# Attention over 16 blocks on one core: four engines' programs as loops with register addresses, and the second half of each V block loaded one block later

## The chip, the cores and the metric

The kernel runs on one core of a Trainium2 chip. Five engines work side by side, each with its own program, and wait for each other only by semaphores: TensorE (PE in the profile) multiplies, VectorE (DVE) transposes, reduces and takes reciprocals, ScalarE (ACT) computes activations (exponentials and scaled copies), GpSimd (POOL) clears a buffer, SyncE (SP) issues transfers. PEld is TensorE's loading of weights. Sixteen DMA engines move data between HBM and the on-chip memory (SBUF); TensorE writes to PSUM, whose banks hold 512 float32 for each of 128 partitions.

The metric is the time of one execution in microseconds, as the device measures it. A profiled execution also has a span, from its first instruction to its last.

## The reference

```python
B, H, Sq, Skv, Dh = 8, 16, 16, 2048, 256
def reference(q, k, v):                    # bfloat16; q: (8,16,16,256), k and v: (8,16,2048,256)
    scale = q.shape[-1] ** -0.5
    scores = jnp.einsum('bhqd,bhkd->bhqk', q, k) * scale
    attn = _softmax(scores, axis=-1)
    return jnp.einsum('bhqk,bhkd->bhqd', attn, v)
```

There are 128 heads. Each has 16 queries and its own 2048 keys and values of 256 numbers, so K and V are 134 MB each, and every byte of them is used by 16 queries only. Q and the output are 1 MiB each.

## The kernel before, in words

**Tiling.** Eight heads make a block g, 0 to 15; their 8 x 16 queries are the 128 rows of the block's scores. Four heads make a unit: block g has units e = 0 and 1. A unit of K or V is 8192 rows of 256 numbers, 64 rows in a line for each of 128 partitions, so its load, K(g,e) or V(g,e), is 4 MiB in 128 runs of 32 KiB (`load`, L97). The tensor SL has four slots of that size, called KA, KB, VA, VB. K(0,0) and K(0,1) are put into VA and VB, all other K into KA and KB; V goes into VA and VB, but for block 15, whose V goes into KA and KB, in two pieces and in eight.

**The steps for one block**, with the names that are used below:
- T(g,e): VectorE transposes unit e of K in place, seen as float32 pairs, in blocks of 32 x 32 (L154, four instructions; two of them are a half unit).
- QK(g,e): TensorE multiplies the unit by the scaled queries, 32 products of 128 x 512 in two groups of 16, one for each half of the unit (`qk`, L234 with a load of weights and L235 without). Both units add into the same four banks, S_ps. The weights QW hold the queries of a unit's four heads at those heads' rows and zeros elsewhere; ScalarE writes them (L174, four copies for each block).
- Maximum (VectorE, L156), exponentials with their sums (ScalarE, L206, two halves), transposes of P (VectorE, L162, two halves), sum and reciprocal (VectorE, L164 and L166).
- Copies: ScalarE places the transposed P of one head after the other into PTz, a buffer of zeros (L219, eight copies, four for each unit).
- PV(g,e): TensorE multiplies 64 columns of PTz by the unit of V, 64 products of 128 x 256 (`pv`, L251), into a bank O_ps for each unit.
- Evacuation: ScalarE scales the result by the reciprocal (L180, 64 rows for each unit), and its queue stores 64 KiB (L184).

**Order.** All programs are written out by hand. VectorE runs, for each block, T(g,0), T(g,1), maximum, transposes of P, sum and reciprocal. TensorE runs QK of block 0 and then a loop over g = 1 to 15: QK(g,0), QK(g,1), PV(g-1,0), PV(g-1,1); PV of block 15 follows. ScalarE runs, for block g, the weights of g+1, the exponentials, the evacuations and the store of g-1, and the eight copies of g. Only TensorE's program has a loop; the others are straight code for 16 blocks.

**The queue of loads.** One queue, SyncE's, issues Q, K(0,0), K(0,1), and then for g = 1 to 15: K(g,0), K(g,1), V(g-1,0), V(g-1,1). Each load waits for its slot: K(g,e) until QK(g-1,e) is done (`c_qk`), V(g,e) until PV(g-1,e) is done (`c_pv`); a load that waits holds up all behind it. Since K(0) lies in VA and VB, K(1) can be issued at once, and V(0,e) waits for QK(0,e).

Of the kernel before, what the change touches and what calls it, by code (L numbers as in the profile page):

```python
# [4 lines left out]
ACTF = mybir.ActivationFunctionType  # L5
ALU = mybir.AluOpType
AX = mybir.AxisListType
PE = mybir.EngineType.PE
BF16 = mybir.dt.bfloat16
# [3 lines left out]
KA, KB, VA, VB = 0, 1, 2, 3  # L13


def bass_standalone__softmax_full_bidir__sampling_kernel(
# [17 lines left out]
    qh = q.rearrange("b h s d -> (b h) (s d)")  # L34
    oh = out.rearrange("b h s d -> (b h s) d")

    with ExitStack() as es:
# [5 lines left out]
        PTc = ec(nc.sbuf_tensor("PTc", [128, T, 32], BF16))  # L43
        PTz = ec(nc.sbuf_tensor("PTz", [128, 2, T, 128], BF16))
        O_fin = ec(nc.sbuf_tensor("O_fin", [128, 2, D], BF16))
        negm = ec(nc.sbuf_tensor("negm", [128, G], F32))
        lsum = ec(nc.sbuf_tensor("lsum", [128, G, 2], F32))
        ltot = ec(nc.sbuf_tensor("ltot", [128, G], F32))
        rinv = ec(nc.sbuf_tensor("rinv", [128, G], F32))

        S_ps = ec(nc.psum_tensor("S_ps", [128, 4, 512], F32))
        O_ps = ec(nc.psum_tensor("O_ps", [128, 4, 512], F32))
# [4 lines left out]
        s_q = sem("s_q")  # L57
        s_k = [sem("s_ka"), sem("s_kb")]
        s_k0 = [sem("s_k0a"), sem("s_k0b")]
        s_v = [sem("s_va"), sem("s_vb")]  # L60
        s_st = [sem("s_st%d" % i) for i in range(2)]
# [4 lines left out]
        c_kt = [[sem("c_kt%d%d" % (e, h)) for h in range(2)] for e in range(2)]  # L66
        c_qk = [sem("c_qka"), sem("c_qkb")]
# [5 lines left out]
        c_pv = [sem("c_pv0"), sem("c_pv1")]  # L73
        c_pl = sem("c_pl")
# [4 lines left out]
        def ap_of(t_ap, offset, dims):  # L79
            return bass.AP(tensor=t_ap.tensor, offset=offset, ap=[list(t_ap.ap[0])] + [list(d) for d in dims])  # L80


        TAIL = [(0, 19), (19, 14), (33, 10), (43, 7), (50, 5), (55, 4), (59, 3), (62, 2)]
        TAIL_A = [(0, 37), (37, 27)]
        s_tail = [sem("s_t%d" % i) for i in range(len(TAIL))]
        s_vl = [sem("s_vl%d" % i) for i in range(len(TAIL_A))]
        s_vc = sem("s_vc")
        s_kl = sem("s_kl")

        def obank(g, e):  # L90
            return e + (2 if g == last else 0)

        def kslot(g, e):
            return (VA, VB)[e] if g == 0 else (KA, KB)[e]
# [3 lines left out]

        def on_sync(eng):
            eng.dma_start(QT[:], qh).then_inc(s_q, 16)  # L100
            for e in range(2):
                load(eng, ku, 0, e, kslot(0, e), 0, T, s_k0[e])
            for g in range(1, G):
                for e in range(2):
                    if g >= 2:
                        eng.wait_ge(c_qk[e], g)
                    if (g, e) != (last, 1):
                        load(eng, ku, g, e, kslot(g, e), 0, T, s_k[e])
                    else:
                        load(eng, ku, g, e, kslot(g, e), 0, 32, s_k[e])  # L110
                        load(eng, ku, g, e, kslot(g, e), 32, 32, s_kl)
                w = g - 1
                for e in range(2):
                    if w:
                        eng.wait_ge(c_pv[e], w)
                    else:
                        eng.wait_ge(c_qk[e], 1)
                    if (w, e) != (last - 1, 1):
                        load(eng, vu, w, e, (VA, VB)[e], 0, T, s_v[e])
                        if e:  # L120
                            eng.sem_inc(s_vc, 16)
                    else:
                        load(eng, vu, w, e, VB, 0, 32, s_v[e])
                        load(eng, vu, w, e, VB, 32, 32, s_vc)

            eng.wait_ge(c_qk[0], G)
            for (a, n), s in zip(TAIL_A, s_vl):
                load(eng, vu, last, 0, KA, a, n, s)
            eng.wait_ge(c_qk[1], G)
            for (a, n), s in zip(TAIL, s_tail):  # L130
                load(eng, vu, last, 1, KB, a, n, s)
            eng.wait_ge(c_ev, 2 * last + 2)
            eng.dma_start(oh[128 * last:128 * last + 128, :], O_fin[:, last % 2, :]).then_inc(s_fin, 16)
            eng.wait_ge(s_fin, 16)

        def on_gpsimd(eng):
            eng.memset(PTz[:].rearrange("p a t c -> p (a t c)").bitcast(F32), 0.0).then_inc(c_pool, 1)  # L137

        def on_vector(eng):
# [4 lines left out]
            for g in range(G):  # L144
                for e in range(2):
                    for c in range(4):
                        if g == 0 and c == 0:
                            eng.wait_ge(s_k0[e], 16)
                        elif c == 0:
                            eng.wait_ge(s_k[e], 16 * g)  # L150
                        elif (g, e, c) == (last, 1, 2):
                            eng.wait_ge(s_kl, 16)
                        x = SLf[:, kslot(g, e), 16 * c:16 * c + 16, :].rearrange("p t i -> p (t i)")
                        eng.transpose(x, x).then_inc(c_kt[e][c // 2], 1)  # L154
                eng.wait_ge(c_qk[1], g + 1)
                eng.tensor_reduce(out=negm[:, g:g + 1], in_=S_ps[:].rearrange("p c n -> p (c n)"),  # L156
                                  axis=AX.X, op=ALU.max, negate=True).then_inc(c_mx, 1)
                for h in range(2):
                    eng.wait_ge(c_ex[h], g + 1)
                    if g and h == 0:  # L160
                        eng.wait_ge(c_cp, 8 * g)
                    eng.transpose(PTc[:, 32 * h:32 * h + 32, :].rearrange("p t x -> p (t x)"),  # L162
                                  P_sb[:, 1024 * h:1024 * h + 1024]).then_inc(c_pt, 1)
                eng.tensor_reduce(out=ltot[:, g:g + 1], in_=lsum[:, g, :], axis=AX.X, op=ALU.add).then_inc(c_ri, 1)  # L164
                eng.wait_ge(c_ri, 2 * g + 1)
                eng.reciprocal(rinv[:, g:g + 1], ltot[:, g:g + 1]).then_inc(c_ri, 1)  # L166

        def on_scalar(eng):
            def qwb(g):
                Q, r = g // 4, g % 4  # L170
                for a in range(4):
                    dv = QW[32 * a:32 * a + 32, 0, 16 * a, :]
                    sv = QT[32 * Q:32 * Q + 32, :]
                    eng.activation(ap_of(dv, dv.offset, [[1024 + 512, 2], [2, 64], [1, 2]]),  # L174
                                   ap_of(sv, sv.offset + 2 * (8 * r + a), [[8, 2], [64, 64], [1, 2]]),
                                   ACTF.Copy, scale=scale).then_inc(c_qw, 1)

            def evac(g, e):
                rows = slice(64 * e, 64 * e + 64)
# [6 lines left out]
            def finish(g):  # L186
                eng.wait_ge(c_ri, 2 * g + 2)
                if g >= 2:
                    eng.wait_ge(s_st[g % 2], 16 * (g // 2))
# [128 lines left out]
```

## Time and profile before

| | us |
|---|---|
| median of 3 runs | 635.95 (635.76 to 636.34) |
| profiled execution | 636.1 |
| its span | 634.8 |
| PE busy | 488.3 (77%) |
| VectorE busy | 365.2 (58%) |
| ScalarE busy | 214.8 (34%) |
| DMA | 270.64 MB, 426 GB/s over the span |

In a row of the timeline stand start and length in us, engine, line, operation, what it writes and reads, the number of instructions put together, and in square brackets how long the engine was idle before and what ended that. A row of windows has the stretch, its length, the busy time of PE, PEld, DVE, ACT and POOL with the number of instructions, TensorE's granted clock, the mean busy share of the 16 DMA engines, and GB/s. A row of the issues of DMA ends with the KB of one transfer and the us from its issue to its landing. In a row of queues stand packets, MB and share of time. SPq is SyncE's queue of transfers.

### The profile page before, as it was taken

The page shows a single profiled execution, that of the slowest core. Times are in us where ns is not written, and L with a number is a line of the kernel's source. Part 1 is how long each engine was busy: PE and PEld are TensorE (multiplying, and loading weights), DVE is VectorE, ACT ScalarE, POOL GpSimd, SP SyncE. Part 2 cuts the span into 40 slices and gives each one's busy share as a digit, 9 for nine tenths or more (in the row PEclk, how much of TensorE's full clock was granted, in tenths as well). Part 3 has the DMA queues.
Part 4 walks back from the last instruction along what each step waited for, and adds up shares of the span by engine and source line. Part 5 has one row for each costly group of instructions (what it writes and reads, how often), then busy time and mean ns, then how long its engine had stood idle before and what let it go on. Part 6 is the DMA issues. An engine that isn't in the chain of part 4 may idle for free.

```text
span 634.8 us, 6396 instructions
## 1 busy us (share of the span) xinstructions
PE 488.3 (77%) x3072; PEld 274.9 (43%) x2560; DVE 365.2 (58%) x210; ACT 214.8 (34%) x289; POOL 7.1 (1%) x5
## 2 busy tenths in 40 slices
PE   0738989595896958869597795967959689595998
PEld 0202828154271532716336262452724527144287
DVE  2968583763738546294562945739366393663830
ACT  1042252525035250342513325142252322524170
POOL 4000000000000000000000000000000000000000
PEclk9978999798997989969799797998979989798899
DMA  8999999999999999999999999999999999999997
GB/s 376 436 441 432 428 432 432 430 430 431 432 429 434 429 432 433 429 434 429 433 430 429 432 429 433 430 430 433 434 429 436 433 433 432 432 432 425 430 425 285
DMA packets 13113, 270.64 MB, mean 426 GB/s; under 512 B 1456, under 2 KB 3760, under 8 KB 4400
## 3 DMA queue, kind: packets, MB, share of 16 engines
q1 hardware_dynamic: 10944, 269.55, 98.8%
q10 hardware_dynamic: 2160, 0.98, 0.5%
q8 instruction: 3, 0.05, 0.0%
q14 instruction: 6, 0.05, 0.0%
HBM read 269.48 MB, written 1.05 MB: 426 GB/s over the span
## 4 chain that ended last, share of the span: by engine, by line
DMA 58%; PE 23%; DVE 16%; ACT 2%; issue 0%; SPq 0%
DMA SL<-in_k_dram 58%; DVE SL L154 15%; PE S_ps L234 11%; PE S_ps L235 10%; PE O_ps L251 2%; ACT PTz L219 1%; DVE PTc L162 1%; DVE negm L156 1%; ACT P_sb L206 0%; ACT O_fin L180 0%; SPq L97 0%; SPq L100 0%; DVE rinv L166 0%; DVE ltot L164 0%
## 5 line engine op out<-in xcount | busy, mean ns | idle before, releaser
L154 DVE STREAM_TRANSPOSE SL<-SL 128x2048 f32<-128x2048 f32 x128 | 284.2, 2279 | 157.9 <-DMA SL<-in_k_dram 157.9
L234 PE MATMUL S_ps<-SL,QW 128*128 128x512 bf16 x512 | 214.0, 418 | 143.5 <-DVE SL L154 143.3
L251 PE MATMUL O_ps<-SL,PTz 128*128 128x256 bf16 x2048 | 226.3, 273 | 0.9 <-ACT PTz L219 0.7
L234 PEld LDWEIGHTS S_ps<-SL,QW 128*128 128x128 bf16 x512 | 75.1, 147 | 326.6 <-issue 171.7
L251 PEld LDWEIGHTS O_ps<-SL,PTz 128*128 128x128 bf16 x2048 | 199.8, 98 | 30.9 <-issue 4.5
L235 PE MATMUL S_ps<-SL,QW 128*128 128x512 bf16 x512 | 212.5, 415 | 0.0
L219 ACT ACTIVATE PTz<-PTc 32x1024 bf16<-32x1024 bf16 x128 | 134.9, 1054 | 11.3 <-ACT O_fin L180 5.9
L174 ACT ACTIVATE QW<-QT 32x256 bf16<-32x256 bf16 x64 | 26.8, 419 | 243.3 <-PE S_ps L235 236.2
L156 DVE TENSOR_REDUCE negm<-S_ps 128x1 f32<-128x2048 f32 x16 | 36.7, 2292 | 61.4 <-PE S_ps L235 61.4
L180 ACT ACTIVATE O_fin<-O_ps,rinv 64x256 bf16<-64x256 f32 x32 | 15.0, 468 | 137.6 <-PE O_ps L251 137.5
L162 DVE STREAM_TRANSPOSE PTc<-P_sb 128x1024 bf16<-128x1024 bf16 x32 | 37.9, 1224 | 20.3 <-ACT P_sb L206 20.3
L206 ACT ACTIVATE P_sb<-S_ps,negm 128x1024 bf16<-128x1024 f32 x32 | 35.3, 1109 | 25.5 <-DVE negm L156 25.5
L137 POOL MEMSET PTz<- 128x8192 f32 x1 | 6.9, 6924 | 0.3 <-POOLq L303 0.3
L206 ACT ACTIVATION_READ_ACCUMULATOR P_sb<-S_ps,negm 128x1 f32 x32 | 6.3, 196 | 0.0
L143 DVE STREAM_TRANSPOSE QT<-QT 128x2048 f32<-128x2048 f32 x1 | 2.3, 2312 | 3.7 <-DMA QT<-in_q_dram 3.7
L166 DVE RECIPROCAL rinv<-ltot 128x1 f32<-128x1 f32 x16 | 2.6, 164 | 0.5
L164 DVE TENSOR_REDUCE ltot<-lsum 128x1 f32<-128x2 f32 x16 | 1.8, 112 | 0.0
L174 ACT ACT_TABLE_LOAD x1 | 1.3, 1283 | 0.7 <-PEq L303 0.7
L140 DVE MEMSET QW<- 128x1024 f32 x1 | 0.9, 912 | 1.0 <-PEq L303 1.0
L303 POOL MEMSET const-bfloat16-1.0<- 128x1 bf16 x1 | 0.1, 101 | 0.0
L303 POOL MEMSET const-uint8-127<- 128x1 uint8 x1 | 0.1, 101 | 0.0
L303 POOL MEMSET const-float32-0.0<- 128x1 f32 x1 | 0.1, 98 | 0.2 <-issue 0.2
(1 smaller groups left out, 0.1 us busy)
## 6 DMA issues: line engine op xcount, KB each, us to landing
SL<-in_k_dram SPq DMA_DIRECT2D x31, 4096.0 KB, 25.8
SL<-in_v_dram SPq DMA_DIRECT2D x29, 4096.0 KB, 29.1
SL<-in_k_dram SPq DMA_DIRECT2D x2, 2048.0 KB, 23.7
SL<-in_v_dram SPq DMA_DIRECT2D x2, 2048.0 KB, 29.2
SL<-in_v_dram SPq DMA_DIRECT2D x1, 2368.0 KB, 21.6
SL<-in_v_dram SPq DMA_DIRECT2D x1, 1728.0 KB, 25.4
SL<-in_v_dram SPq DMA_DIRECT2D x1, 1216.0 KB, 20.7
QT<-in_q_dram SPq DMA_DIRECT2D x1, 1024.0 KB, 4.9
```

What stands on the lines that cost most here:

```text
L137: eng.memset(PTz[:].rearrange("p a t c -> p (a t c)").bitcast(F32), 0.0).then_inc(c_pool, 1)
L154: eng.transpose(x, x).then_inc(c_kt[e][c // 2], 1)
L156: eng.tensor_reduce(out=negm[:, g:g + 1], in_=S_ps[:].rearrange("p c n -> p (c n)"), axis=AX.X, op=ALU.max, negate=True).then_inc(c_mx, 1)
L162: eng.transpose(PTc[:, 32 * h:32 * h + 32, :].rearrange("p t x -> p (t x)"), P_sb[:, 1024 * h:1024 * h + 1024]).then_inc(c_pt, 1)
L166: eng.reciprocal(rinv[:, g:g + 1], ltot[:, g:g + 1]).then_inc(c_ri, 1)
L174: eng.activation(ap_of(dv, dv.offset, [[1024 + 512, 2], [2, 64], [1, 2]]), ap_of(sv, sv.offset + 2 * (8 * r + a), [[8, 2], [64, 64], [1, 2]]),
L180: eng.activation(O_fin[rows, g % 2, :], O_ps[rows, obank(g, e), 0:D], ACTF.Copy, scale=rinv[rows, g:g + 1]).then_inc(c_ev, 1)
L206: eng.activation(P_sb[:, 1024 * h:1024 * h + 1024], S_ps[:, 2 * h:2 * h + 2, :].rearrange("p c n -> p (c n)"), ACTF.Exp, bias=negm[:, g:g ...
L219: eng.activation(PTz[32 * a:32 * a + 32, z, :, 64 * e + 16 * a:64 * e + 16 * a + 16], sv[:, :, 16 * (a % 2):16 * (a % 2) + 16], ACTF.Copy) ...
L234: return eng.matmul(dst, w, x, start=start, stop=stop)
L235: return eng.add_instruction(mybir.InstMatmult(name=nc.get_next_instruction_name(), engine=PE, start_tensor_calc=start, stop_tensor_calc=stop,
L251: ins = eng.matmul(O_ps[:, bank, 0:D], PTz[:, z, t, :], SL[:, slot, t, :], start=(t == 0), stop=(t == T - 1))
```

## The change

- SyncE, ScalarE and VectorE get loops over the blocks (`nc.Fori`), with addresses and the values of waits computed in registers, and branches (`If_ne`, `If_lt`) for what the first or last block does otherwise. GpSimd gets increments that raise some semaphores at the start, so that one formula serves all blocks. TensorE keeps one loop for all of its work after QK of block 0, now with PV inside for every block; QK of block 0 is two nested loops with 8 products in a round, after four products that clear S_ps with the zeroed PTz as both operands. QK(0,0) and QK(0,1) each wait for the whole of T.
- T takes two instructions for a unit instead of four.
- Q is loaded with other rows on the partitions: partition 32a + u holds head 4u + a, so that ScalarE can address a block's queries with one register. The source's dimensions are 4 x 32 x 4096 instead of 128 x 4096.
- V's second unit goes one block later: the queue's order is K(j,0), K(j,1), V(j-2,1), V(j-1,0), and TensorE's is QK(r,0), QK(r,1), PV(r-2,1), PV(r-1,0). For j = 2 there is no V(0,1) to issue (it was issued before), so that K(2,0), K(2,1), V(1,0) and K(3,0) follow each other.
- Both units of PV now add into one bank, and one evacuation of 128 rows follows PV(g,1). PV(g+1,0) waits for it. ScalarE's order is: weights of the next block, exponentials of g, evacuation of g-2, copies of unit 1 of g-1, store of g-2, copies of unit 0 of g. VectorE's transposes of P of block g wait for the copies of unit 1 of g-1, since PTc is one buffer. VectorE's order in a round is: maximum, transposes of P, sum and reciprocal of g, then T of g+1.
- V(14,1), V(15,0) and V(15,1) are loaded in 3, 2 and 8 pieces, all into VA and VB; each piece waits until PV has passed its columns, counted in steps of 16 columns. Results stay in O_fin for all blocks.

```diff
-KA, KB, VA, VB = 0, 1, 2, 3
+VA, VB, KA, KB = 0, 1, 2, 3
+C = 16
...
-    qh = q.rearrange("b h s d -> (b h) (s d)")
+    qh = q.rearrange("b h s d -> (b h) (s d)").rearrange("(u a) n -> a u n", a=4)
...
+        PIECES = {(last - 1, 1): [(0, 16), (16, 14), (30, 34)], (last, 0): [(0, 37), (37, 27)],
+                  (last, 1): [(0, 16), (16, 14), (30, 11), (41, 8), (49, 6), (55, 4), (59, 3), (62, 2)]}
...
+        def k_and_v(eng, j, es):
+            for e in range(2):
+                eng.wait_ge(c_qk, 8 * j + 4 * e - 4)
+                load(eng, ku, j, e, KA + e, 0, T, s_k[e])
+            for e in es:
+                w = j - 1 - e
+                eng.wait_ge(c_pv, 8 * w + 4 * e + 4)
+                load(eng, vu, w, e, VA + e, 0, T, s_v[e])
...
         def on_sync(eng):
             eng.dma_start(QT[:], qh).then_inc(s_q, 16)
...
+            for j in range(2, 3):
+                k_and_v(eng, j, (0,))
+            with nc.Fori(3, last, engines=[SP]) as j:
+                k_and_v(eng, j, (1, 0))
...
         def on_vector(eng):
...
+            for e in range(2):
+                eng.wait_ge(s_k0[e], 16)
+                for h in range(2):
+                    kt(e, h, VA + e)
+            with nc.Fori(0, G, engines=[DVE]) as g:
+                eng.wait_ge(c_qk, 8 * g + 8)
...
                 for h in range(2):
                     eng.wait_ge(c_ex[h], g + 1)
-                    if g and h == 0:
-                        eng.wait_ge(c_cp, 8 * g)
+                    if h == 0:
+
+                        eng.wait_ge(c_cp, 8 * g + 9)
...
+                with eng.If_lt(gg, last):
+                    for e in range(2):
+                        for h in range(2):
+                            if h == 0:
+                                eng.wait_ge(s_k[e], 16 * g + 16)
+                            elif e:
+                                eng.wait_ge(s_kl, 16 * ((g + 2) >> 4) + 1)
+                            kt(e, h, KA + e)
...
         def on_scalar(eng):
...
+            with nc.Fori(0, G, engines=[ACT]) as g:
+                eng.wait_ge(c_qk, 8 * g + 8)
+                qwb((g + 1) & 15)
                 eng.wait_ge(c_mx, g + 1)
...
+                with eng.If_ne(g2, 0):
+                    evac(n)
+                with eng.If_ne(gg, 0):
+                    eng.wait_ge(c_pv, 8 * g)
+                    copies(1)
+                with eng.If_ne(g2, 0):
+                    store(n, (g + 14) & 15)
                 eng.wait_ge(c_pt, 2 * g + 2)
+                eng.wait_ge(c_pv, 8 * g + 4)
+                copies(0)
...
         def on_tensor(eng):
...
+            with nc.Fori(0, 2, engines=[PE]) as e:
+                with nc.Fori(0, 4, engines=[PE]) as b:
+                    eng.wait_ge(c_kt, 2 * e + 2)
+                    for par in range(2):
+                        for c in range(4):
+                            ins = mm(S_ps[:, c, :], QW[:, e, :, 2 * b + par], SLk[:, VA + e, c, b, par, :, :],
+                                     False, False, c == 0, False)
+                    ins.then_inc(c_qk, 1)
...
+            with nc.Fori(1, G + 2, engines=[PE]) as r:
+                rr = eng.to_reg(r)
+                with eng.If_lt(rr, G):
+                    for e in range(2):
+                        for h in range(2):
+                            eng.wait_ge(c_kt, 4 * r + 2 * e + h + 1)
+                            if e + h == 0:
+                                eng.wait_ge(c_ex[1], rr)
+                            ins = qk(e, (2 * h, 2 * h + 1), KA + e)
+                        ins.then_inc(c_qk, 4)
+                with eng.If_ne(rr, 1):
...
+                    eng.wait_ge(c_cp, 8 * r + 1)
+                    eng.wait_ge(s_v[1], 16 * (r - 1))
+                    pv(1, lambda t: lim2 if t in dict(PIECES[(last - 1, 1)]) else lim1)
+                with eng.If_lt(rr, G + 1):
+                    lim = eng.to_reg((r & 16) + 1)
+                    eng.wait_ge(c_ev, rr)
+                    eng.wait_ge(c_cp, 8 * r + 5)
+                    eng.wait_ge(s_v[0], 16 * r)
+                    pv(0, lambda t: lim)
```

258 lines of the change are left out of this document (98 added, 160 removed).

## The prediction

> K(g,e), V(g,e), T, QK, PV, "copies" and "evacuation" are the loads and steps named in the section on the kernel before.
>
> **What bounds the kernel now.** I read the page first, then long and short windows, the queue's waits, one block's timeline, the start and the end.
>
> ```profile
> span 634.8 us, 6396 instructions
> ...
> PE 488.3 (77%) x3072; PEld 274.9 (43%) x2560; DVE 365.2 (58%) x210; ACT 214.8 (34%) x289; POOL 7.1 (1%) x5
> ...
> q1 hardware_dynamic: 10944, 269.55, 98.8%
> ...
> q8 instruction: 3, 0.05, 0.0%
> ...
> DMA 58%; PE 23%; DVE 16%; ACT 2%; issue 0%; SPq 0%
> ```
>
> The queue that brings K and V (q1) is busy 98.8% of the span, and no engine is over 77%. In the chain of waits (last line) most of the time is one transfer after another.
>
> ```profile
> 100.00:600.00 500.00, 392.35 (x2456) 219.74 (x2046) 291.90 (x168) 171.54 (x230) 0.00 (x0) 0.90 1.00 431
> 631.00:631.50 0.50, 0.50 (x7) 0.45 (x5) 0.00 (x0) 0.00 (x0) 0.00 (x0) 1.00 0.08 29
> ```
>
> Through the middle 500 us all 16 DMA engines are busy (share 1.00, the column before the last) at 431 GB/s, 27 for each. So a 4 MiB load takes 4.194 MB / 431 GB/s = 9.73 us and a block (four loads, 38.9, and its store) 39.0. The second row says that by 631.5 the stream has nearly run out.
>
> ```profile
> SPq L97 <- PE S_ps L235: 392.1, 32, 25.8
> SPq L97 <- PE O_ps L251: 185.9, 28, 7.0
> ```
>
> The issuing queue waits long (total, times, longest), but that costs nothing while loads issued earlier still move. The time is therefore: first byte, stream, any time in which all four slots are taken and nothing moves, and what follows the last byte.
>
> ```profile
> 346.37 8.61 ACT L219 ACTIVATE PTz<-PTc 32x1024 bf16<-32x1024 bf16 x8 [0.41 <-ACT O_fin L180]
> 347.91 8.89 DVE L154 STREAM_TRANSPOSE SL<-SL 128x2048 f32<-128x2048 f32 x4 [10.23 <-DMA SL<-in_k_dram]
> ...
> 362.54 8.31 SPq L97 DMA_DIRECT2D SL<-in_k_dram  x2
> ...
> 370.32 14.13 PE L251 MATMUL O_ps<-SL,PTz 128*128 128x256 bf16 x128
> ...
> 370.52 2.29 DVE L156 TENSOR_REDUCE negm<-S_ps 128x1 f32<-128x2048 f32 x1 [3.84 <-PE S_ps L235]
> ...
> 374.08 2.37 DVE L162 STREAM_TRANSPOSE PTc<-P_sb 128x1024 bf16<-128x1024 bf16 x2 [1.27 <-ACT P_sb L206]
> ...
> 376.53 0.16 DVE L166 RECIPROCAL rinv<-ltot 128x1 f32<-128x1 f32 x1
> ...
> 377.59 0.47 ACT L180 ACTIVATE O_fin<-O_ps,rinv 64x256 bf16<-64x256 f32 x1 [2.44 <-PE O_ps L251]
> ```
>
> One block (start and length in us). T takes 8.89 for a unit; VectorE is idle 10.23 before it, because K arrives late, not the engine. From the end of QK (370.52) to the evacuation (377.59) are 7.07, the 64 products of a unit's PV.
>
> **The change part by part.**
>
> *Q's load.* Its source was 128 rows in one dimension and becomes 4 x 32 rows, with the 4 outermost. In the kernel before q1 carries 76 transfers (74 loads, Q, the last store) of 128 rows each: 76 x (128 + 16) = 10944, the count above. So each is one packet for a row and one closing packet for each of 16 engines: rows are dealt out along the outermost dimension. No row shows an outermost 4. One end of its price is nothing:
>
> ```profile
> QT<-in_q_dram SPq DMA_DIRECT2D x1, 1024.0 KB, 4.9
> ...
> 0.00:1.70 1.70, 0.00 (x0) 0.00 (x0) 0.68 (x1) 0.96 (x1) 1.17 (x5) 1.00 0.00 0
> 1.70:2.50 0.80, 0.00 (x0) 0.00 (x0) 0.23 (x1) 0.32 (x1) 0.80 (x1) 1.00 0.71 143
> ...
> 0.74 0.38 SPq L100 DMA_DIRECT2D QT<-in_q_dram  x1
> ```
>
> The other end is 4 engines: 1.049 MB at 4 x 27 GB/s = 9.7 us where 16 take 2.4, so +7.3 for all that is queued behind it on those four. I take 7.3, since 4 entries can't be dealt to 16 engines in the way that the count shows. A load has landed when its slowest engine has, so K(0,0) comes 7.3 later. (The issue at 0.74 and the empty first window give about 1.0 us from issue to first byte.) [...]
>
> *First products.* QK(0,0) began after half of its unit; now it waits for the whole unit, in two nested loops of 8 products a round.
>
> ```profile
> 15.34 8.89 DVE L154 STREAM_TRANSPOSE SL<-SL 128x2048 f32<-128x2048 f32 x4 [7.39 <-DMA SL<-in_k_dram]
> ...
> 19.99 0.62 PE L234 MATMUL S_ps<-SL,QW 128*128 128x512 bf16 x1 [19.99 <-DVE SL L154]
> 20.41 0.63 PE L235 MATMUL S_ps<-SL,QW 128*128 128x512 bf16 x1
> ...
> 25.05 8.89 DVE L154 STREAM_TRANSPOSE SL<-SL 128x2048 f32<-128x2048 f32 x4 [0.82 <-DMA SL<-in_k_dram]
> ...
> 37.78 2.29 DVE L156 TENSOR_REDUCE negm<-S_ps 128x1 f32<-128x2048 f32 x1 [3.84 <-PE S_ps L235]
> ...
> 42.21 0.20 ACT L206 ACTIVATION_READ_ACCUMULATOR P_sb<-S_ps,negm 128x1 f32 x1
> ...
> 43.87 17.64 DVE L154 STREAM_TRANSPOSE SL<-SL 128x2048 f32<-128x2048 f32 x8
> ```
>
> Before: T(0,0) from 15.34, first product 19.99, T(0,1) to 33.94, QK(0,1) done 37.78, that is 3.84 later.
>
> ```profile
> 74.79 8.90 DVE SL L154 x4
> 83.69 0.05 issue
> ...
> 84.18 0.22 PE S_ps L235
> ...
> 87.51 26.38 DMA SL<-in_k_dram
> ```
>
> [...] Now T(0,0) runs 22.6 to 31.5, and QK(0,0) takes 9 x 0.42 + 23 x 0.22 = 8.8, to 40.3, or 40.7 with 0.1 for each of four loop ends. T(0,1) runs 32.35 to 41.25; QK(0,1) takes the 3.84 of a half, 16 x 0.22 for the other and 0.4 for loop ends: done at 49.0. Loop ends aren't in the trace: nothing to 0.38 each (the queue's issue at 0.74 is the nearest instruction without data), which gives 48.6 to 50.8. The four products that clear the scores and GpSimd's increments come before K(0,0) and are hidden by it.
>
> *V's second unit one block later.* After V(0,1) the queue has K(2,0), K(2,1), V(1,0) and then K(3,0): three loads instead of four ahead of K(3,0), since V(1,1) waits for PV(0,1), now behind QK(2,1). And the copies of unit 1 move from the end of their block to behind the next block's exponentials, ahead of its transposes of P, which T waits for on VectorE. From QK(0,1) done: T(1,0) 43.87 - 37.78 = 6.1, and 0.2 for a branch; T of both units 17.64; half of QK 3.84: QK(1,1) at +27.8. Maximum and exponentials 42.41 - 37.78 = 4.6; branches 0.2; four copies 4.3 (half of 8.61); transposes of P 2.4; sums and a branch 0.5: T(2,0) at +39.8 = 88.8. QK(2,0) ends 12.7 (74.79 to 87.51) to 14.6 (347.91 to 362.54) after T begins; with the middle, 13.7, at 102.5. There K(3,0) is issued; first byte 103.5.
>
> ```profile
> 72.32 0.33 SPq L97 DMA_DIRECT2D SL<-in_v_dram  x1
> ...
> SL<-in_v_dram SPq DMA_DIRECT2D x1, 4096.0 KB, 22.1
> ```
>
> The ninth load, V(1,0), landed at 72.32 + 22.1 = 94.4; with Q's delay at 101.7. Its last byte moves 0.9 sooner (K(0,0): 15.34 less 1.7, less 5.24 MB at 431 GB/s, less 0.5 for the weak second window). From 100.8 all four slots are full, with K(2,0), K(2,1), V(1,0) and V(0,1), and the stream stands still: 2.7 us. The bounds 48.6 with 12.7 and 50.8 with 14.6 give 1.3 and 5.4. Everything later shifts by 7.3 + 2.7 = 10.0, on all engines: the twelve that Q didn't delay only stand longer.
>
> *Later blocks.* T(3,0) comes at +76.6 = 125.6, QK(3,0) ends at 139.3, K(4,0)'s first byte is at 140.3; the stream has work until 103.5 + 38.9 = 142.4. Room 2.1, so no second stall. The loop of dependences is now T 17.64, half of QK 3.84, PV 7.07, evacuation 0.47, branches 0.3, copies 4.3, transposes of P 2.4, sums and branch 0.5: 36.5 us. Against 39.0 it gains 2.5 a block on K(3,0)'s lead (landed 114.1, used 125.6) and waits for data from about block 8. Some 15 register instructions and branches lie on it; they may cost 2.5 / 15 = 0.17 us each beyond my 0.05 (the "issue" piece at 83.69) before they bind. Looping on ScalarE, VectorE and the queue costs nothing while this room lasts, and its whole length in each of 12 blocks without it (rival D). Waits added beside this path: PV(g-1,0) waits for the evacuation of block g-2 (one bank now), so PE is done at 370.5 + 7.07 + 0.65 + 7.07 = 385.3, and next has a half unit of K at 386.9 + 4.4 (the next block begins 39.0 after 347.91): hidden by 6. Behind PV(g-1,0) ScalarE's copies of unit 0 end at 389.6, its next work is at 409.5. One evacuation of 128 rows for two of 64 saves 0.47 where ScalarE was idle: nothing.
>
> *The end.*
>
> ```profile
> 582.41 17.66 DVE L154 STREAM_TRANSPOSE SL<-SL 128x2048 f32<-128x2048 f32 x8 [10.26 <-DMA SL<-in_k_dram]
> ...
> 618.53 14.15 PE L251 MATMUL O_ps<-SL,PTz 128*128 128x256 bf16 x128 [0.69 <-ACT PTz L219]
> ...
> 632.71 0.47 ACT L180 ACTIVATE O_fin<-O_ps,rinv 64x256 bf16<-64x256 f32 x1 [6.44 <-PE O_ps L251]
> ```
>
> Before: 128 products from 618.53 to 632.68, behind the stream's end; 2.1 us of evacuation and store follow, to 634.8. Now K(15) is a load earlier and the products wait for their piece of V: last byte 631.4, landed 0.4 later (an estimate, half of the 0.9, for a small piece), last products 0.4, then 2.1: 634.3, so -0.5. PE's own chain, with T(15,0) at 582.41 - 9.73 and 17.8 for both units: 590.5 + 3.84 + 5 x 7.07 + 0.65 for each of two evacuations = 631.0, hidden by the data, barely; uncovered, the -0.5 shrinks to 0.
>
> *Sum.* 634.8 + 7.3 + 2.7 - 0.5 = 644.3 of span. The profiled execution took 636.1, 1.3 outside its span: 645.6. The median of the runs, 635.95, is 0.15 lower, which I leave out.
>
> **The rivals.**
>
> B: Q still runs on 16 engines. Only the stall and the end remain: 636.1 + 2.7 - 0.5 = 638.3. For it: the 4.9 us. Against it: the 4 in front.
>
> C, not slower: the stream never stands still. It decides at K(3,0)'s issue: before 92.5 without Q's delay, so QK(0,1) done by 92.5 - 53.5 = 39.0, 1.2 after the old 37.78. Starting QK(0,0) at half a unit would nearly do it; waiting for whole units can't by the rows above, and Q at 16 engines is needed too. 636.1 - 0.5 = 635.6; it is faster by more than a measurement can tell only if the uneven last microsecond of the stream goes as well, somewhat under half of its chance.
>
> D: the loops' own instructions bind every block. At 0.3 us for each of 15 the loop of dependences is 36.0 + 4.5 = 40.5; from 125.6 twelve of them end at 612, where K(15,0) landed at 582.7: +29, so 675. For it: only PE had a loop before. Against it: PE's loop goes round 15 times here, and its instruction queue (q8) moved 3 packets in all. [...]
>
> **How the numbers follow.** A, the forecast, 0.74; B 0.11; C 0.07; D 0.08. A's own range: Q 7.3 +- 0.6, stall 1.3 to 5.4, end -0.5 to 0, so 643.6 to 649.4. The range takes in B, and a weak D above: 637.5 to 651; C and most of D are left out. 0.2% is 1.3 us, about what a measurement of this kernel can tell from no change. Faster 0.03 and same 0.04 are C; slower 0.93 is the rest.
>
> **What would show it.** Q landing near 13 instead of 5.6, and 77 x 144 - 12 = 11076 packets on q1 (one load is cut into one piece more; Q has 12 closing packets fewer). T(0,0) at 22.6; QK(0,1) done at 49; a hole of about 3 us in DMA between 100 and 105, and none later; VectorE waiting some 2 us for K in the late blocks; the end 2.9 us after the last piece. The prediction is wrong if Q lands before 6 (B), if there is no hole (C), or if VectorE never waits for K in late blocks (D).

## The result and the profile after

| | before | after |
|---|---|---|
| median of 6 runs each | 636.06 us (635.76 to 636.34) | 663.76 us (663.06 to 664.64) |
| ratio after / before | | 1.0436, 95% interval 1.0423 to 1.0449 |
| profiled execution, its span | 636.1, 634.8 | 664.4, 662.9 |

The change makes the kernel 27.7 us slower; 9.7 were forecast. The page of the kernel after, engines, queues and the chain of waits:

```profile
span 662.9 us, 7353 instructions
...
PE 497.0 (75%) x3076; PEld 271.6 (41%) x2545; DVE 361.0 (54%) x146; ACT 209.1 (32%) x277; POOL 7.1 (1%) x5
...
q1 hardware_dynamic: 11076, 269.55, 97.0%
...
q8 instruction: 1, 0.02, 0.0%
...
DMA 42%; PE 33%; DVE 18%; issue 4%; ACT 3%; ACTq 1%; SPq 0%; DVEq 0%
```

PE is busy 9 us longer than before, the other engines no longer, the same bytes move, and q1 has the 11076 packets that were forecast, so Q does run on four engines. The start is another matter. VectorE's timeline of the kernel after:

```profile
30.40 2.31 DVE L145 STREAM_TRANSPOSE QT<-QT 128x2048 f32<-128x2048 f32 x1 [28.46 <-DMA QT<-in_q_dram]
39.85 8.77 DVE L149 STREAM_TRANSPOSE SL<-SL 128x4096 f32<-128x4096 f32 x2 [7.15 <-DMA SL<-in_k_dram]
...
66.29 2.29 DVE L157 TENSOR_REDUCE negm<-S_ps 128x1 f32<-128x2048 f32 x1 [7.96 <-PE S_ps L244]
```

Q lands at 30.4 (forecast: near 13) and T(0,0) starts at 39.85, 24.5 us later than the 15.34 of before. The windows of the first 30 us say what happens meanwhile, first of the kernel after, then of the kernel before (the last two numbers are the DMA engines' busy share and GB/s):

```profile
2.00:5.00 3.00, 0.00 (x0) 0.00 (x0) 0.00 (x0) 0.02 (x1) 3.00 (x1) 1.00 0.91 183
5.00:10.00 5.00, 0.00 (x0) 0.00 (x0) 0.00 (x0) 0.00 (x0) 3.60 (x1) 1.00 1.02 210
10.00:15.00 5.00, 0.00 (x0) 0.00 (x0) 0.00 (x0) 0.00 (x0) 0.00 (x0) 1.00 1.11 193
15.00:20.00 5.00, 0.00 (x0) 0.00 (x0) 0.00 (x0) 0.00 (x0) 0.00 (x0) 1.00 1.12 177
20.00:25.00 5.00, 0.00 (x0) 0.00 (x0) 0.00 (x0) 0.00 (x0) 0.00 (x0) 1.00 0.87 136
25.00:30.00 5.00, 0.00 (x0) 0.00 (x0) 0.00 (x0) 0.00 (x0) 0.00 (x0) 1.00 0.92 288
```

```profile
2.00:5.00 3.00, 0.00 (x0) 0.00 (x0) 0.00 (x0) 0.02 (x1) 3.00 (x1) 1.00 1.02 415
5.00:10.00 5.00, 0.00 (x0) 0.00 (x0) 2.31 (x1) 1.65 (x4) 2.65 (x1) 1.00 1.02 439
10.00:15.00 5.00, 0.00 (x0) 0.00 (x0) 0.00 (x0) 0.00 (x0) 0.00 (x0) 1.00 1.06 459
```

All engines count as busy (share about 1), yet in the first 25 us less than half of the bytes move. In the trace a packet of Q (8 KB) takes 0.84 us in the median where it took 0.31, and a packet of K (32 KB), on the twelve engines that don't carry Q, takes 2.4 us at first and 3.3 later where it took 1.21. So a busy share of about 1 stood beside 210 GB/s here and beside 439 before (5 to 10 us): it doesn't tell a working engine from one that is held up; GB/s beside it does.

From there the kernel after does nearly what was forecast. SyncE's timeline and the windows around K(3,0), then VectorE's waits, then the second half of its transposes of P in three blocks, VectorE's waits for K in later ones, and the last evacuation:

```profile
120.31 7.39 SPq L95 DMA_DIRECT2D SL<-in_k_dram  x2
```

```profile
116.00:118.00 2.00, 2.00 (x11) 0.59 (x5) 2.00 (x1) 0.00 (x0) 0.00 (x0) 1.00 0.61 262
118.00:119.50 1.50, 1.50 (x8) 0.56 (x4) 1.50 (x2) 0.00 (x0) 0.00 (x0) 1.00 0.05 22
119.50:121.30 1.80, 1.80 (x9) 0.58 (x4) 1.80 (x1) 0.00 (x0) 0.00 (x0) 1.00 0.07 18
121.30:125.00 3.70, 3.70 (x18) 1.15 (x8) 1.76 (x1) 0.00 (x0) 0.00 (x0) 1.00 1.13 416
```

```profile
DVE PTc L164 <- ACT PTz L202: 142.7, 15, 9.7
DVE SL L149 <- DMA SL<-in_k_dram: 34.0, 20, 7.1
```

```profile
140.40 1.20 DVE L164 STREAM_TRANSPOSE PTc<-P_sb 128x1024 bf16<-128x1024 bf16 x1
...
176.40 1.20 DVE L164 STREAM_TRANSPOSE PTc<-P_sb 128x1024 bf16<-128x1024 bf16 x1
...
212.40 1.20 DVE L164 STREAM_TRANSPOSE PTc<-P_sb 128x1024 bf16<-128x1024 bf16 x1
...
259.40 8.77 DVE L149 STREAM_TRANSPOSE SL<-SL 128x4096 f32<-128x4096 f32 x2 [0.67 <-DMA SL<-in_k_dram]
...
288.67 8.77 DVE L149 STREAM_TRANSPOSE SL<-SL 128x4096 f32<-128x4096 f32 x2 [1.95 <-DMA SL<-in_k_dram]
...
366.67 8.77 DVE L149 STREAM_TRANSPOSE SL<-SL 128x4096 f32<-128x4096 f32 x2 [1.96 <-DMA SL<-in_k_dram]
...
660.75 0.47 ACT L195 ACTIVATE O_fin<-O_ps,rinv 128x256 bf16<-128x256 f32 x1 [11.70 <-PE O_ps L260]
```

The scores of block 0 are complete at 66.29, K(3,0) is issued 54.0 later, and up to 121.3 next to nothing moves: the hole lies where it was forecast, once shifted by Q's extra 17.2. The blocks behind it follow each other in 36.0 us. At 259.40, in block 6, VectorE waits for K again for the first time, and from block 7 (288.67) on it waits 1.9 to 2.0 us at the start of each block, so that blocks follow in the stream's 39.0. Over the whole run it waits less for K than before (34.0 us instead of 157.9) and more for ScalarE's copies (142.7), at no cost: the stream has the longer step.

Landings in the trace give the whole account against before. K(0,0): +24.5. V(1,0), the ninth load: 119.64 instead of 94.55, +25.1. The tenth: K(3,0) at 132.53, before V(1,1) at 104.17, +28.4. The last piece of V: 660.27 instead of 631.81, +28.5. The end: 2.6 us after it instead of 3.0, so +28.1 in span.

### The profile page after: what moved, and what is told of

The parts are those of the page before. It is cut to its first block, busy times and chain, and to the rows that moved or that the text cites. A ratio compares the mean times of both kernels' runs of the same rounds, so it can differ in the third digit from the quotient of the medians.

```text
span 662.9 us, 7353 instructions
## 1 busy us (share of the span) xinstructions
PE 497.0 (75%) x3076; PEld 271.6 (41%) x2545; DVE 361.0 (54%) x146; ACT 209.1 (32%) x277; POOL 7.1 (1%) x5
## 3 DMA queue, kind: packets, MB, share of 16 engines
q1 hardware_dynamic: 11076, 269.55, 97.0%
## 4 chain that ended last, share of the span: by engine, by line
DMA 42%; PE 33%; DVE 18%; issue 4%; ACT 3%; ACTq 1%; SPq 0%; DVEq 0%
DMA SL<-in_k_dram 40%; DVE SL L149 16%; PE S_ps L244 13%; PE S_ps L243 12%; PE O_ps L260 8%; ACT PTz L202 3%; DMA SL<-in_v_dram 2%; DVE PTc L164 1%; DVE negm L157 1%; ACTq L207 0%; ACT P_sb L217 0%; ACT O_fin L195 0%; SPq L107 0%; SPq L95 0%; DVEq L155 0%
## 5 line engine op out<-in xcount | busy, mean ns | idle before, releaser
L149 DVE STREAM_TRANSPOSE SL<-SL 128x4096 f32<-128x4096 f32 x64 | 280.0, 4420 | 34.2 <-DMA SL<-in_k_dram 34.0
L243 PE MATMUL S_ps<-SL,QW 128*128 128x512 bf16 (+1 forms) x496 | 210.5, 424 | 114.2 <-DVE SL L149 114.1
L260 PE MATMUL O_ps<-SL,PTz 128*128 128x256 bf16 x2048 | 229.1, 273 | 15.0 <-ACT O_fin L195 13.2
L244 PE MATMUL S_ps<-SL,QW 128*128 128x512 bf16 (+1 forms) x528 | 217.4, 422 | 0.0
L243 PEld LDWEIGHTS S_ps<-SL,QW 128*128 128x128 bf16 (+1 forms) x496 | 72.9, 147 | 305.3 <-issue 180.2
L189 ACT ACTIVATE QW<-QT 32x256 bf16 (+1 forms) x68 | 28.6, 420 | 345.3 <-PE S_ps L244 313.4
L164 DVE STREAM_TRANSPOSE PTc<-P_sb 128x1024 bf16<-128x1024 bf16 x32 | 37.9, 1224 | 144.1 <-ACT PTz L202 142.7
L243 PE MATMUL S_ps<-PTz 128*128 128x512 bf16 x1 | 0.6, 609 | 34.5 <-ACT QW L189 34.5
L195 ACT ACTIVATE O_fin<-O_ps,rinv 128x256 f32 (+1 forms) x16 | 7.6, 474 | 50.3 <-PE O_ps L260 50.3
L145 DVE STREAM_TRANSPOSE QT<-QT 128x2048 f32<-128x2048 f32 x1 | 2.3, 2311 | 28.5 <-DMA QT<-in_q_dram 28.5
L168 DVE RECIPROCAL rinv<-ltot 128x1 f32 x16 | 2.6, 164 | 2.1
L244 PE MATMUL S_ps<-PTz 128*128 128x512 bf16 x3 | 1.5, 634 | 0.0
## 6 DMA issues: line engine op xcount, KB each, us to landing
SL<-in_k_dram SPq DMA_DIRECT2D x31, 4096.0 KB, 25.1
```

What stands on the lines that cost most here:

```text
L149: eng.transpose(x, x).then_inc(c_kt, 1)
L168: eng.reciprocal(rinv[:, bass.ds(g + 1, 1)], ltot[:]).then_inc(c_ri, 1)
L189: eng.activation(dv, sv, ACTF.Copy, scale=scale).then_inc(c_qw, 1)
L195: eng.activation(O_fin[:, n, :], O_ps[:, 0:D], ACTF.Copy, scale=rinv[:, bass.ds(n, 1)]).then_inc(c_ev, 1)
L243: return eng.matmul(dst, w, x, start=start, stop=stop, skip_group_check=not check)
L244: return eng.add_instruction(mybir.InstMatmult(name=nc.get_next_instruction_name(), engine=PE, start_tensor_calc=start, stop_tensor_calc=stop,
```

## The experiments

Labels that begin with "before" are the kernel before with what the diff shows altered, those with "after" the changed kernel in the same way. Packet durations and landings are from the traces. An experiment that ran once has its time here, one that ran several times also the ratio to the kernel before (636.0 to 636.1 on the same chips). In each, "T(0,0) at" is the start of the first transposes of K.

**Is it Q's load, and nothing else?** One run puts the new load of Q into the kernel before; two take it out of the kernel after.

```diff
 before_q4 (and ScalarE's fixed addresses in QT to match)
-    qh = q.rearrange("b h s d -> (b h) (s d)")
+    qh = q.rearrange("b h s d -> (b h) (s d)").rearrange("(u a) n -> a u n", a=4)
 after_q16
-            eng.dma_start(QT[:], qh).then_inc(s_q, 16)
+            for a in range(4):
+                eng.dma_start(QT[32 * a:32 * a + 32, :], qh[a]).then_inc(s_q, 16)
 after_plain
-    qh = q.rearrange("b h s d -> (b h) (s d)").rearrange("(u a) n -> a u n", a=4)
+    qh = q.rearrange("b h s d -> (b h) (s d)")
```

> The kernel before, with only Q's placement of the change (one transfer, 4 x 32 rows, the same places) and the addresses that go with it, in straight code. Theory: K(0,0)'s transposes begin near 39.8 instead of 15.3; no stall before K(3,0) beyond that, since the old order keeps one more load ahead; 636.1 + 24.5 = 660.6. Rival (another part of the change makes the start late): at most Q's own 7 us, 643.5 or less.

> The changed kernel, with Q loaded in four transfers of 32 rows each to the same places, so that each has 32 in front and runs on 16 engines. Nothing is left out. Theory (all of the late start is Q's load on four engines): K(0,0)'s transposes begin at about 15.5 us instead of 39.85, QK(0,1) is done 26.4 later at 42, the stream stands still about 3 us before K(3,0) as in the changed kernel, and the time is 663.8 - 24.4 = 639.4. Rival (the start is late for another reason, for instance the loops' set-up or GpSimd's increments): K(0,0) still comes after 30 us and the time stays above 655.

> The changed kernel with Q loaded as in the kernel before, in one transfer on 16 engines in Q's own order; the heads then stand on other partitions than the changed kernel takes them for, so queries meet the keys of other heads, with the same work. My theory: all that the change costs beside Q's load is the late second unit of V and the whole units of the first products: transposes of K from 15.3, scores of block 0 complete 26.4 later at 41.8, K(3,0) issued 54 after that at 95.8, 3.3 after the stream would want it, the end 0.4 nearer to the last piece: 635.95 + 3.1 - 0.4 = 638.6, ratio 1.004. Rival: part of the 27.7 us is in the loops (slower blocks, hidden by data only while the stream is ahead): 642 or more. Rival C of the prediction: the stream never stands still: 635.6.

Measured: before_q4 660.29 us (ratio 1.0371, 1.0354 to 1.0388), T(0,0) at 39.67; after_q16 641.26 (1.0089, 1.0072 to 1.0106), T(0,0) at 17.54; after_plain 639.36 (1.0048, 1.0032 to 1.0065), T(0,0) at 15.37, with the heads of Q on partitions that the kernel takes for others. VectorE's timeline of before_q4, and SyncE's of after_plain:

```profile
30.20 2.31 DVE L143 STREAM_TRANSPOSE QT<-QT 128x2048 f32<-128x2048 f32 x1 [28.27 <-DMA QT<-in_q_dram]
39.67 8.89 DVE L154 STREAM_TRANSPOSE SL<-SL 128x2048 f32<-128x2048 f32 x4 [7.16 <-DMA SL<-in_k_dram]
```

```profile
61.98 7.78 SPq L95 DMA_DIRECT2D SL<-in_k_dram  x2
...
95.68 7.39 SPq L95 DMA_DIRECT2D SL<-in_k_dram  x2
```

Q's load alone makes 24.2 us in the kernel before, without a loop or a moved transfer. With Q loaded as before, the rest of the change costs 3.3 us, at the place forecast: K(3,0) is issued at 95.68 (expected 95.8), and its landing is 3.8 late. The time is 0.8 above the 638.6 expected; the landings put 0.9 us on a first gap, ahead of K(2,0), which the expectation had left out. after_q16 was no clean undoing of Q's term: T(0,0) stayed 2.2 late, although all 16 engines worked (q1 has 11136 packets, 60 more than in the kernel after: 16 closing packets for each of the four transfers in place of 4 for the one). That was the first sign that the number of engines is not the whole matter.

**Is it K beside Q, or the rows?** In one run K waits until Q has landed; in the other Q keeps its own order of rows, and is cut into 124 and 4 rows so that four engines carry it (q1 then has 10936 packets, 8 under the 10944 of before: 2 x 4 closing packets in place of 16).

```diff
 after_q_alone
             eng.dma_start(QT[:], qh).then_inc(s_q, 16)
+            eng.wait_ge(s_q, 16)
 before_q124
-            eng.dma_start(QT[:], qh).then_inc(s_q, 16)
+            eng.dma_start(QT[0:124, :], qh[0:124, :]).then_inc(s_q, 16)
+            eng.dma_start(QT[124:128, :], qh[124:128, :]).then_inc(s_q, 16)
```

> The changed kernel, with the queue waiting for Q to land before it issues K(0,0). If Q's four engines and K's twelve slow each other (they run side by side in the changed kernel), Q alone takes 32 packets x 0.31 us = 9.9 and lands near 13, K(0,0) lands 12 later near 25.5, and the time falls by about 14 to 650. If the four engines are slow by themselves with these rows, Q still lands near 28 to 30, K(0,0) near 42, and the time is about 666.

> The kernel before, with Q in the old places but cut into 124 rows and 4 rows, neither divisible by more than four engines up to 16; each engine then reads consecutive rows of 8 KiB. If any transfer on four engines beside K's slows all packets, K(0,0) comes near 39 and the time is about 660. If the slowing needs the change's interleaved rows (four engines reading neighbouring rows in step), packets keep 0.31 and 1.21 us, K(0,0) comes at 22.6 and the time is about 643.

Measured: after_q_alone 656.62 us, T(0,0) at 33.02; before_q124 654.95, T(0,0) at 34.45. VectorE's timeline of after_q_alone and a window of it, then a window of before_q124:

```profile
20.76 2.31 DVE L146 STREAM_TRANSPOSE QT<-QT 128x2048 f32<-128x2048 f32 x1 [18.82 <-DMA QT<-in_q_dram]
```

```profile
10.00:15.00 5.00, 0.00 (x0) 0.00 (x0) 0.00 (x0) 0.00 (x0) 0.00 (x0) 1.00 0.26 69
```

```profile
10.00:15.00 5.00, 0.00 (x0) 0.00 (x0) 0.00 (x0) 0.00 (x0) 0.00 (x0) 1.00 1.04 203
```

Neither value expected of after_q_alone came out (650 or 666). With nothing beside them the four engines (share 0.26 of 16) carry 69 GB/s, not 4 x 27; their packets take either 0.31 or about 0.61 us, with little between. Consecutive rows don't mend it either: before_q124 moves 203 GB/s with all engines busy, and its time lies between the 643 and the 660 expected. So neither K nor the order of the rows is the whole cause. The durations of 0.31 and about 0.61 made the author guess that two engines take turns at something, which no trace shows.

**Which partitions are written together?** The author's guess, theory P in what follows, was that some partitions make a group, and that engines that write one group at the same time share its rate. No trace shows which engine writes which partitions, or which of them make a group. The test has 16 engines and fewer partitions at a time.

```diff
 before_q64
+            for a in range(2):
+                eng.dma_start(QT[64 * a:64 * a + 64, :], qh[64 * a:64 * a + 64, :]).then_inc(s_q, 16)
 before_q8
+            for a in range(4):
+                eng.dma_start(QT[32 * a:32 * a + 32, :],
+                              qh[32 * a:32 * a + 32, :].rearrange("(e i) n -> e i n", i=4)).then_inc(s_q, 16)
```

> The kernel before with Q loaded in two transfers of 64 consecutive rows: all 16 engines work, four rows each, read in order; nothing else differs. Theory P (partitions): in the kernel before each engine writes 8 partitions of its own (8 KB packet 0.31 us); a transfer to half of the partitions puts two engines on each group of partitions at a time, and the group, not the engine, sets the rate, as in the 32-row pieces (0.6 us a packet with 16 engines). Then packets take about 0.6 us, Q lands near 8 and the first transposes of K start near 17.5, 2.2 later than before; one look gives about 638. Rival R (reads): packets are slow where an engine's rows are not consecutive or where few engines work, and here neither holds: 0.31 us, transposes from 15.3, 636. [...]

> The kernel before with Q loaded in four transfers of 32 rows, each cut into eight times four rows, so that eight engines carry it, one to each group of partitions. [...] Rival F (few engines): packets are slow because fewer than 16 engines carry Q: 0.65 to 0.95 and 2.4 and more from the first packet on, Q lands near 15, transposes start near 26, one look gives 647.

Measured: before_q64 638.16 us, T(0,0) at 17.54, packets 0.61 in the median; before_q8 637.9, T(0,0) at 17.14, packets 0.60. The row of before_q64 and the queue of before_q8:

```profile
17.54 8.89 DVE L155 STREAM_TRANSPOSE SL<-SL 128x2048 f32<-128x2048 f32 x4 [7.31 <-DMA SL<-in_k_dram]
```

```profile
q1 hardware_dynamic: 10992, 269.55, 98.9%
```

before_q64 came out at theory P's numbers: 16 engines (q1 has 10960 packets, 16 closing packets more than before) and consecutive rows, and still twice the time for a packet. 16 packets of 8192 bytes in 0.607 us are 216 GB/s, half of the stream's 431. before_q8 tested nothing of what it was made for: the queue's 10992 packets (10944 and 3 x 16 closing packets more) show 16 engines. Its rows are one run in memory, and the author takes it that its dimensions were joined for that. It only repeats the halved rate.

**Four engines, each on eight neighbouring partitions.** By the source's dimensions every fourth row of 32 goes to one engine, onto eight neighbouring partitions. The queue's 10944 packets, in four transfers for Q instead of one, show four engines for each (4 x (32 + 4) = 128 + 16).

```diff
 before_q4d; before_q4d_alone has the last line too
+            for a in range(4):
+                eng.dma_start(QT[32 * a:32 * a + 32, :],
+                              qh[32 * a:32 * a + 32, :].rearrange("(i e) n -> e i n", e=4)).then_inc(s_q, 16)
+            eng.wait_ge(s_q, 64)
```

> The kernel before with Q in four transfers of 32 rows, each on four engines that write eight neighbouring partitions apiece (every fourth row of the 32, so that it isn't joined into one run of rows; heads then stand on other partitions, with the same work), and K's first load held until Q has landed. No two of the four engines write the same group of partitions. Theory P: sharing a group is what made the packets of the changed kernel's Q slow when it moved alone (half of them 0.31 us, half 0.61, median 0.557, landed 20.7); without sharing all take 0.31, 32 of them 9.9 us, and Q lands near 12 to 12.5. This is the 27 GB/s of an engine that the prediction used. Rival F (four engines are slow by themselves): 0.557 us again, Q lands near 20.

> The same Q on four engines with groups of partitions apart, and K's loads not held, so that they move beside it. In the changed kernel K's 32 KB packets took 2.4 to 3.3 us beside Q instead of 1.21, on all twelve other engines. Theory P1: what slowed K is the same sharing, among Q's engines and between them and K's; with Q's engines apart only the sharing with K's engines is left: packets of Q between 0.31 and 0.62, Q lands between 12 and 21, transposes of K start between 22.6 and 31, one look gives 643 to 651. Rival H: it isn't partitions, but rows read by few engines beside a stream of long rows, at the source: Q lands at 26 to 28 and transposes start at 36 to 40 as in the kernels with four engines before: 656 to 660.

Measured: before_q4d_alone 646.44 us, packets 0.31 from the tenth to the ninetieth percentile, the last done at 13.1; before_q4d 650.53, T(0,0) at 29.55. Window and timeline of the first, then of the second:

```profile
5.00:10.00 5.00, 0.00 (x0) 0.00 (x0) 0.00 (x0) 0.00 (x0) 2.66 (x1) 1.00 0.26 110
```

```profile
13.43 2.31 DVE L146 STREAM_TRANSPOSE QT<-QT 128x2048 f32<-128x2048 f32 x1 [11.50 <-DMA QT<-in_q_dram]
```

```profile
10.00:15.00 5.00, 0.00 (x0) 0.00 (x0) 0.00 (x0) 0.00 (x0) 0.00 (x0) 1.00 1.03 233
```

```profile
29.55 8.89 DVE L156 STREAM_TRANSPOSE SL<-SL 128x2048 f32<-128x2048 f32 x4 [7.22 <-DMA SL<-in_k_dram]
```

With the same share of 0.26, four engines now move 110 GB/s instead of 69. They are not slow by themselves: 110 / 4 is the 27 GB/s of an engine again. Nor is it the half of the partitions that decides: here a transfer covers 32 neighbouring partitions, all in one half, and its packets keep 0.31. That agrees with theory P; what its groups are it doesn't show. Beside K, Q's packets start at 0.31, and go to 0.5 to 0.65 as soon as K moves; K's take 2.3 on all twelve other engines. P1's range holds, rival H's doesn't. But K's slowness remained, and with it the question of whether the partitions make it.

**The partitions, or only moving beside K?** Two runs load Q as before and then 128 rows of 8 KB more, on four engines (q1 has 11104 packets, 8 x (16 + 4) more than before), into space that K(1,0) fills later. They differ in the partitions alone. The author chose these by an assumption on which engines write which partitions in K's loads, that no trace shows.

```diff
+            for i in range(8):
+                p0 = (0, 32)[i % 2]               # before_far4: (64, 96)
+                eng.dma_start(SL[p0:p0 + 16, KA, 16 * (i // 2):16 * (i // 2) + 16, :].rearrange("p t d -> p (t d)"),
+                              qh[16 * i:16 * i + 16, :].rearrange("(i e) n -> e i n", e=4)).then_inc(s_d, 16)
...
+                if g == 1:
+                    eng.wait_ge(s_d, 128)
```

> [...] Rival H (short rows on few engines slow K by themselves): K's packets beside them take 2.3 us and the rows 0.5 to 0.9; transposes start after 30, one look gives over 650.

> [...]

Measured: before_own4 646.41 us; before_far4 652.06. Windows and timeline of before_own4, then of before_far4:

```profile
10.00:15.00 5.00, 0.00 (x0) 0.00 (x0) 0.00 (x0) 0.00 (x0) 0.00 (x0) 1.00 0.98 413
```

```profile
25.53 8.89 DVE L161 STREAM_TRANSPOSE SL<-SL 128x2048 f32<-128x2048 f32 x4 [17.70 <-DMA SL<-in_k_dram]
```

```profile
10.00:15.00 5.00, 0.00 (x0) 0.00 (x0) 0.00 (x0) 0.00 (x0) 0.00 (x0) 1.00 0.99 211
15.00:20.00 5.00, 0.00 (x0) 0.00 (x0) 0.00 (x0) 0.00 (x0) 0.00 (x0) 1.00 0.99 208
```

```profile
31.17 8.89 DVE L161 STREAM_TRANSPOSE SL<-SL 128x2048 f32<-128x2048 f32 x4 [23.25 <-DMA SL<-in_k_dram]
```

The pair settles that the partitions matter. The same rows, sizes and number of engines beside the same stream: 413 GB/s in before_own4, 211 in before_far4. In before_own4 the extra rows take 0.31 us and K's packets, but for the first of each engine, 1.21: rival H is out. In before_far4 they take 0.62 and 2.44 once both move side by side, and K's 2.44 hold for all twelve engines; the first half of the extra rows still took 0.31. That four engines share something with K's writers in the one run and not in the other is the author's reading; which engine wrote which partitions stands in no trace.

**The rest of the cost, and a way back.** The scores of block 0 wait for whole units in the kernel after; here they begin at half a unit again. The second run also splits Q over two queues, which is meant to have both halves of the partitions written at once.

```diff
 after_q16_halves: after_q16, and QK of block 0 as
+            for e in range(2):
+                for h in range(2):
+                    eng.wait_ge(c_kt, 2 * e + h + 1)
+                    for bp in range(8):
+                        for c in (2 * h, 2 * h + 1):
+                            ins = mm(S_ps[:, c, :], QW[:, e, :, bp], SLk[:, VA + e, c, bp // 2, bp % 2, :, :],
+                                     False, False, c == 2 * h, False)
+                ins.then_inc(c_qk, 4)
 after_2q_halves: that, with the pieces a = 2 and 3 of Q issued by ScalarE's queue
```

> The changed kernel with Q in four transfers of 32 rows on 16 engines, as in the run before of that kind (641.3), and the products of block 0 written out and begun after half a unit, as in the kernel before, instead of after whole units. My theory: the scores of block 0 are complete 3.9 us after the last transpose instead of 7.9, so K(2,0) and K(3,0) are issued 4 us earlier; the stream's two standstills there (1.9 and about 1.6 us) go, and 2.2 us for Q's slower load stay: 635.95 + 2.2 - 0.4 = 637.8, or 638.0. Rival: the standstills come from the wait of K(3,0) behind the late second unit of V alone, whenever block 0 ends: 641 as it was.

> The changed kernel with products of block 0 begun at half a unit and Q in four transfers of 32 rows on 16 engines, but two of them (partitions 0 to 63) on SyncE's queue and two (64 to 127) on ScalarE's at the same time. Theory P: the two queues take turns on each engine, both halves of the partitions are written at once, and Q's packets come back toward 0.31 to 0.45 us: Q lands between 5.6 and 6.6, transposes of K start between 15.3 and 16.5, and the time is 635.7 to 636.8. Rival: as with four pieces in one queue (637.9, transposes from 17.3), as the pieces or the engines are what is slow, not the halves.

Measured: after_q16_halves 637.90 us (ratio 1.0034, 1.0020 to 1.0049); after_2q_halves 637.84 (1.0032, 1.0020 to 1.0044). A window of after_q16, the same of after_q16_halves, and the row of after_2q_halves:

```profile
85.00:100.00 15.00, 12.08 (x48) 3.50 (x24) 15.00 (x4) 2.41 (x3) 0.00 (x0) 0.80 0.86 350
```

```profile
85.00:100.00 15.00, 14.38 (x62) 4.29 (x30) 11.44 (x3) 0.00 (x0) 0.00 (x0) 0.95 0.99 422
```

```profile
16.71 8.77 DVE L150 STREAM_TRANSPOSE SL<-SL 128x4096 f32<-128x4096 f32 x2 [7.41 <-DMA SL<-in_k_dram]
```

In after_q16_halves the hole between 85 and 100 is gone (0.99 busy instead of 0.86), though V's second unit still comes a block later. The gap ahead of K(2,0) is gone too: against after_q16, K(2,0) lands 1.4 us sooner and K(3,0) 3.0, and the time is 3.4 less. What is left over the kernel before is Q's late landing, T(0,0) at 17.30, and nothing of the loops. The two queues gave less than was hoped: Q's packets take 0.31 at first, then 0.4 to 0.55 (0.44 in the median instead of 0.60), and T(0,0) starts at 16.71, just outside the 15.3 to 16.5 expected. The time is above the 635.7 to 636.8 expected; its six runs spread from 637.03 to 639.01, and it can't be told from that with one queue. Neither version beats the kernel before, and the runs point to none that would by more than the 0.35 us that the end gained.

## Why the prediction was wrong

The direction was right, and so were the four engines, the hole and the end. The step that failed is one term of the sum, *Q's load*: it was forecast at +7.3 and measured at +24.5, since both the rate that it gave the four engines and its overlap with K's stream were wrong.

- *Q's load.* "The other end is 4 engines: 1.049 MB at 4 x 27 GB/s = 9.7 us where 16 take 2.4" took the rate of an engine from the full stream, in which a packet of K takes 1.21 us, and held that the other twelve engines are untouched (they "only stand longer"); their packets went from 1.21 us to 2.4 and 3.3. The four engines are shown by the 11076 packets; the rate wasn't. The runs take the 24.5 apart: four engines at 0.31 us a packet cost 7.4 to 7.8 (24 packets of 0.31 more for each by before_q4d_alone; 25.53 - 15.34 - 2.4 by before_own4); the same four beside K, each on eight neighbouring partitions at a time, cost 14.2 (before_q4d, T(0,0) at 29.55); beside K and with Q's rows as the change places them, 24.3 (before_q4, 39.67). The forecast had the first part alone, and called the 4-engine case "the other end", though nothing in the trace bounded it from above.
- *First products.* Forecast 26.4 from T(0,0) to the scores of block 0; measured 66.29 - 39.85 = 26.4. Of its terms, 0.42 and 0.22 are the distances of products in the trace of before: the first nine 0.42, then 0.22, at a granted clock of 1.00 in both stretches (19.99 to 24, 24 to 30); why the first are slower no run shows. Loop ends cost nearly the 0.1 us that was assumed: the last rounds of 8 products begin 1.82 to 1.86 apart, where 8 x 0.22 are 1.76.
- *V's second unit one block later.* K(3,0) was forecast 53.5 after the scores of block 0 and came at 54.0; the stand-still was forecast at 2.7, and the tenth load lost 28.4 - 25.1 = 3.3. The 0.6 before it, a gap ahead of K(2,0), was missing from the sum. after_q16_halves shows that the late V costs nothing once the first products begin at half a unit: it is the two together.
- *Later blocks.* Forecast 36.5 us for the loop of dependences; measured 36.0. VectorE waits 1.95 for K in the late blocks, as "some 2 us" said, and from block 7 on, where "about block 8" was forecast; behind K(3,0) there is no second hole.
- *The end.* Forecast -0.5; measured -0.35 (2.6 us after the last piece instead of 3.0).
- Rival B (Q on 16 engines) didn't happen, but its 638.3 is what after_plain, 639.36, comes near to, 1 us over it for the gap ahead of K(2,0) and the longer hole. Rival C failed at both of its conditions; its remedy, the half unit, does away with the hole. Rival D is out: no block is bound by its loops' instructions, and q8 moved 1 packet instead of 3.

The sum against the profiled execution, 664.4 instead of 645.6: 17.2 too little for Q, 0.6 for the gap, 0.6 for the hole, 0.1 for the last landing, 0.15 for the end, and 0.2 more outside the span.

## What to carry to other kernels

Before an access pattern of a transfer is altered, write down how many engines will carry it and which partitions they will write. The count alone doesn't set the rate: four engines moved 110 GB/s in before_q4d_alone and 69 in after_q_alone, and the partitions alone decided whether 128 more rows and the stream beside them moved at 413 GB/s or at 211 (before_own4, before_far4). A short transfer at the start of a stream is priced by what it does to the stream, not by its own bytes: Q's 1 MiB cost 24.2 us in before_q4. Read GB/s beside the busy share: about 1 went with 439 GB/s in the kernel before, and with 210 in the kernel after.

## What the runs showed of the hardware that was not expected

- A packet of 8 KB that takes 0.31 us in the kernel before took 0.61 on 16 engines that wrote 64 partitions in a transfer (before_q64), and about 0.61 for half of the packets of four engines that wrote all 128 (after_q_alone); four engines with 32 partitions in a transfer, eight neighbouring ones each, kept 0.31 (before_q4d_alone). That engines share a rate where they write certain partitions together agrees with this; no trace shows which partitions these are.
- 128 rows of 8 KB on four engines beside K's stream moved with it at 413 GB/s (10 to 15 us) on one choice of partitions and at 211 on another, with K's packets on all twelve other engines at 1.21 and 2.44 us (before_own4, before_far4). In the kernel after, K's packets reach 3.3 us (25 to 30 us). Why all twelve are held up isn't shown by any run here.
- before_q8 ran on 16 engines (10992 packets) although its source was written with 8 in front of rows that are one run in memory; with 4 in front of every fourth row the kernel after ran on four (11076).
